# One fixed order of all steps, three copied index columns per tile and a fourth PT buffer in block-sparse attention followed by a cosine MLP

## The chip, the cores and the metric

The kernel runs on one core of one Trainium2 chip. The metric is the time of one execution on the device in microseconds (us). Before the change the median of three runs is 831.07 us, from 828.74 to 832.98. "PE" is the matrix engine (TensorE), "DVE" VectorE, "ACT" ScalarE, "POOL" GpSimd, and "SP" the queue that issues most DMAs.

## The reference

Inputs are q, k and v with batch 4, 8 heads, 768 positions and 64 columns, the sampled key blocks, and the two MLP weights (float64, 512 by 2048 and 2048 by 512).

```
scores = scale * np.matmul(q, k.transpose(0, 1, 3, 2))
mask = np.abs(blk_i - blk_j) <= 1          # blocks of 32 positions
mask = mask | (blk_i == 0) | (blk_j == 0) | (blk_i == 23) | (blk_j == 23)
# and 3 sampled key blocks for each query block
scores = np.where(mask, scores, -1000000000.0)
attn = np.exp(scores - np.max(scores, axis=-1, keepdims=True))
attn = attn / (np.sum(attn, axis=-1, keepdims=True) + 1e-09)
x = np.matmul(attn, v)                     # heads side by side: 3072 rows of 512
h = x @ w_in
out = (h * np.cos(h)) @ w_out
```

## The kernel before, in words

Each batch is cut into six tiles of 128 query rows. Five are sparse (each head sees 352 keys: its window, the two end blocks, and three sampled blocks per query block). The sixth holds the first and the last three query blocks and is dense (768 keys). Tiles are numbered 0 to 23, so tiles 5, 11, 17 and 23 are dense. Every float32 value is held as two float16 halves, high and low.

`plan_kernel` writes the work as a list of some 3200 named steps; each step issues one or more instructions on one engine. For a tile `n` and a unit `j` (two heads of a sparse tile, one head of a dense one), the steps are these:

- `qk` (PE, lines 1501 to 1518): scores into the one PSUM buffer `sp`. A sparse unit is one step of 24 matmuls; a dense unit is two steps, one for each half of the keys.
- `mx` twice and `nb` (DVE, L1534, L1551): the mask is added and the row maximum taken, for each half of `sp`, into one of four `P` buffers.
- `ex` twice and `ph` (ACT, L1556, L1566): the exponential, and the high float16 half into one of three `ring` buffers. `pl` (DVE, L1570) writes the low half.
- `PT` (SP, L1585): a DMA transpose from `ring` into one of three `PT` buffers.
- `pv` (PE, L1595 and L1607, dense L1621): the product with the values in one of two `V` buffers, into `xp`. It frees the `PT` buffer, and the tile's last one frees `V`.

A `V` buffer of a sparse tile is filled by three SP loads and by four indirect DMAs that POOL issues (`vi`, L1469, 96 rows each); they read the row numbers from a column of `gidx`, which is written once at the start. For every pair of tiles the MLP follows: `m` (PE, L1782, 12 matmuls a step), `ev` (ACT, L1791), `ka`, `kb`, `gm`, `gl` (DVE, L1801 to L1823), `sin` and `gh` (ACT, L1809, L1820), and `d` (PE, L1832, 6 matmuls a step). ACT loads another table whenever it goes from an exponential to a sine or back.

Each engine runs its own steps strictly in the order in which they were written out, and waits where an operand isn't there. In the kernel before that order came out of `Plan.run`: it took the table `POS` as priorities, simulated queues and engines with a cost for each step, and wrote out at each point the step that could start first, with the smaller `POS` among equals. Buffers of a class were handed out in the order of `POS`.

Of the kernel before, what the change touches and what calls it, by code (L numbers as in the profile page):

```python
# [273 lines left out]
class Val:  # L274


    def __init__(self, cls=None, t=None):
        self.cls, self.t, self.slot, self.avail = cls, t, None, 0.0
        self.ops = []
        self.parts = {}  # L280
# [11 lines left out]


class ArrayClock:


    WINDOW, COLD, UP, DOWN = 4096 / 1200.0, 1.85, 0.76, 0.38

# [1615 lines left out]
```

## Time and profile before

| | before |
|---|---|
| median of 3 runs | 831.07 us (828.74 to 832.98) |
| the profiled execution, and its span from the first to the last instruction | 824.2 us, 822.4 us |
| busy PE, DVE, ACT, POOL | 719.6, 641.1, 635.7, 107.4 us |
| DMA, all queues | 146.55 MB |

The profiled execution is one more execution than the three timed ones. Busy times count every instruction from its start to its end; matmuls overlap, so a busy PE isn't a PE at its peak. The granted clock is given as a share of 2.4 GHz; its two levels are 1.2 and 2.4 GHz. The DMA share is the mean busy share of the 16 DMA engines, and it can come out above 1.

### The profile page before, as it was taken

The numbers are of one execution on the slowest core, as the hardware profiler recorded it, in microseconds if no ns is written. First come the engines' busy times: TensorE is split into PE (matmuls) and PEld (weight loads), VectorE is DVE, ScalarE is ACT, GpSimd is POOL, SyncE is SP. The second block draws the span as 40 slices with busy tenths as digits, with TensorE's granted clock in tenths as the row PEclk, the third lists the DMA queues.
The fourth block names the chain that finished last, engine by engine and source line by source line (L and its number), as shares of the span: only waits on it lengthen the run. The fifth ranks groups of instructions, "written<-read, shape, count | busy, mean of one in ns | idle before, by whom it ended". The sixth has DMA issues, their size and how long they took to land.

```text
span 822.4 us, 23028 instructions
## 1 busy us (share of the span) xinstructions
PE 719.6 (87%) x9272; PEld 507.2 (62%) x9272; DVE 641.1 (78%) x1617; ACT 635.7 (77%) x1218; POOL 107.4 (13%) x128
## 2 busy tenths in 40 slices
PE   3537589899889856999999979999999979999998
PEld 2425467566466435767767647767586558577573
DVE  5979999999969763889878975989768957967362
ACT  3667899899868973999969985989679967977251
POOL 6232203000022022100030212000300210200000
PEclk9955689999899986999999998999999989999999
DMA  8999977954989899999997999978977997675100
GB/s 309 325 236 259 239 150 174 212 126 113 205 257 183 157 196 167 171 228 177 270 187 158 178 207 206 202 154 186 217 140 134 196 181 163 157 130 99 26 26 26
DMA packets 270299, 146.55 MB, mean 178 GB/s; under 512 B 241648, under 2 KB 241776, under 8 KB 270192
## 3 DMA queue, kind: packets, MB, share of 16 engines
q1 hardware_dynamic: 265072, 129.35, 74.3%
q0 software_dynamic: 5120, 15.73, 8.6%
q8 instruction: 72, 1.18, 0.6%
q14 instruction: 35, 0.29, 0.1%
HBM read 68.23 MB, written 12.58 MB: 98 GB/s over the span
## 4 chain that ended last, share of the span: by engine, by line
PE 37%; ACT 14%; DMA 13%; DVE 9%; issue 3%; SPq 1%; DVEq 0%; ACTq 0%
PE ph L1782 15%; PE po L1832 14%; DMA PT<-ring 7%; ACT P L1556 4%; PE xp L1607 2%; ACT ring L1566 2%; DMA W<-kn 2%; DMA scr<-n 2%; PE sp L1518 1%; DVE P L1534 1%; DMA qs<-in_q_dram 1%; ACT hs L1791 1%; DVE g L1823 1%; ACT junk L1237 1%; PE xp L1595 1%
## 5 line engine op out<-in xcount | busy, mean ns | idle before, releaser
L1782 PE MATMUL ph<-xT,w 128*128 128x256 f16 x2304 | 272.3, 277 | 8.3 <-ACT hs L1791 4.2
L1832 PE MATMUL po<-w,g 128*128 128x512 f16 x1152 | 265.6, 381 | 4.1 <-DVE kn L1848 1.6
L1782 PEld LDWEIGHTS <-w 128*128 128x128 f16 x2304 | 225.6, 99 | 45.6 <-issue 8.5
L1832 PEld LDWEIGHTS <-g 128*128 128x128 f16 x1152 | 108.7, 98 | 124.4 <-issue 4.1
L1556 ACT ACTIVATE P<-P,sm 128x352 f32<-128x352 f32 (+1 forms) x224 | 152.0, 680 | 32.3 <-DVE sm L1551 23.0
L1469 POOL DMA_INDIRECT V<-scr,gidx x80 | 91.8, 1147 | 595.0 <-PE xp L1595 278.2
L1570 DVE TENSOR_TENSOR ring<-P,ring 128x704 f16<-128x704 f32 (+1 forms) x112 | 100.5, 906 | 23.8 <-ACT ring L1566 22.7
L1534 DVE CUSTOM_DVE_ANT_1 P<-sp,bias 128x352 f32<-128x352 f32 x160 | 78.6, 519 | 35.4 <-PE sp L1507 35.1
L1791 ACT ACTIVATE hs<-ph,sm 128x512 f32<-128x512 f32 x96 | 63.0, 677 | 44.7 <-PE ph L1782 40.8
L1566 ACT CAST ring<-P 128x704 f16<-128x704 f32 (+1 forms) x112 | 86.5, 786 | 13.3 <-DMA PT<-ring 12.7
L1814 DVE SCALAR_TENSOR_TENSOR hs<-hs,sm,g 128x1024 f32<-128x1024 f32 x48 | 61.1, 1281 | 11.8 <-ACT g L1809 11.2
L1501 PE MATMUL sp<-W,U 128*128 128x192 f16 x320 | 52.5, 265 | 13.5 <-DVE sm L1534 10.7
L1823 DVE TENSOR_TENSOR g<-hs,g 128x1024 f16<-128x1024 f32 x48 | 58.6, 1223 | 6.9 <-ACT g L1820 6.8
L1809 ACT ACTIVATE g<-g,sm 128x1024 f32<-128x1024 f32 x48 | 54.7, 1145 | 11.5 <-DVE g L1805 11.2
L1595 PE MATMUL xp<-V,PT 96*32 96x64 f16 x1920 | 30.9, 203 | 35.4 <-DMA PT<-ring 35.4
L1805 DVE SCALAR_TENSOR_TENSOR g<-g,hs 128x1024 f32<-128x1024 f32 x48 | 58.3, 1218 | 0.6 <-DVE Wg L1343 0.2
L1820 ACT ACTIVATE g<-hs 128x1024 f16<-128x1024 f32 x48 | 50.4, 1051 | 8.4 <-DVE hs L1814 7.9
L1801 DVE TENSOR_SCALAR g<-hs 128x1024 f32<-128x1024 f32 x48 | 32.9, 690 | 28.0 <-ACT hs L1791 27.9
L1595 PEld LDWEIGHTS <-PT 96*32 96x32 f16 x1920 | 21.7, 102 | 51.7 <-DMA PT<-ring 43.5
L1502 PE MATMUL sp<-W,U 128*128 128x64 f16 x320 | 47.8, 205 | 0.0
L1607 PE MATMUL xp<-V,PT 128*128 128x64 f16 x960 | 46.6, 204 | 0.0
L1502 PEld LDWEIGHTS <-U 128*128 128x128 f16 x320 | 33.1, 104 | 15.5 <-issue 12.1
(164 smaller groups left out, 919.1 us busy)
## 6 DMA issues: line engine op xcount, KB each, us to landing
V<-scr SPq DMA_DIRECT2D x20, 384.0 KB, 5.1
stage<-in_k_dram SPq DMA_DIRECT2D x12, 512.0 KB
w<-in_moe_w_in_dram SPq DMA_DIRECT2D x12, 512.0 KB, 6.9
w<-in_moe_w_out_dram SPq DMA_DIRECT2D x12, 512.0 KB, 4.4
V<-scr SPq DMA_DIRECT2D x8, 768.0 KB, 6.3
scr<-n SPq DMA_DIRECT2D x21, 256.0 KB, 3.3
qs<-in_q_dram SPq DMA_DIRECT2D x20, 256.0 KB, 3.5
U<-U SPq DMA_DIRECT2D x40, 128.0 KB, 2.9
```

Of the source, the lines that this page charges most:

```text
L1469: self.nc.gpsimd.indirect_dma_start(V[:96, 2 + j, :], None, self.scr[b][:, :], bass.IndirectOffsetOnAxis(ap=self.gidx[:96, c : c + 1], axi ...
L1502: mm(spv[:, :, 96:128].rearrange("p y (n c) -> p y n c", c=hf), u, ends, start=False, stop=False)
L1534: self.nc.vector.tensor_tensor_reduce(out=self.p_view(n, Pt)[:, a].rearrange("p (n c) -> p n c", c=hf), in0=sp[:, :w].rearrange("p (n c) - ...
L1556: self.nc.scalar.activation(Pv[:, a], Pv[:, a], AF.Exp, scale=qc[:, 4:5], bias=nb[:, bcol : bcol + 1], accum_out=sums[:, 2 * j + a : 2 * j ...
L1566: self.nc.scalar.copy(R[:, :, 0, : self.width(n)], self.p_view(n, Pt))
L1570: self.nc.vector.tensor_tensor(R[:, :, 1, :w], self.p_view(n, Pt), R[:, :, 0, :w], ALU.subtract)
L1607: mm(xp[:, h, :], PT[:, 6 * a + 3 * l + c, :], V[:, c, h, d0:d1], start=False, stop=(a == 1 and c == 1 and x == len(terms) - 1),)
L1782: self.nc.tensor.matmul(ph[:, ff, :], self.W1[p][:, wl, cc, c * P : (c + 1) * P], xT[:, xl * NCC + cc, :], start=(j == 0), stop=(j == len( ...
L1791: self.nc.scalar.activation(hs[:, h * 512 : h * 512 + 512], ph.rearrange("p f t -> p (f t)"), AF.Copy, scale=self.turns[b][:, p : p + 1])
L1814: self.nc.vector.scalar_tensor_tensor(hs, hs, c[:, p : p + 1], kt, op0=ALU.mult, op1=ALU.mult)
L1823: self.nc.vector.tensor_tensor(g[:, 1024:2048], hs, g[:, 0:1024], ALU.subtract)
L1832: self.nc.tensor.matmul(po, g[:, gl, ff, t * P : (t + 1) * P], self.W2[p][:, wl, ff, :], start=(first and ff == half * hf and j == 0), sto ...
```

## The change

Four things change.

The planner's simulation is gone. `POS` now holds whole numbers, one for each of the 3262 steps, and `Plan.run` sorts the steps by them: that is the order, and a buffer that a step needs is the free one of its class that was freed longest ago. The table is new throughout.

Of a sparse tile's four gathers, three (`vi` 1 to 3) no longer read their row numbers from `gidx`. A new DVE step `gr` copies that column into a column of a new tile `gone`, one per gather, and the gather reads it there; so it waits for the copy. There are 60 such copies.

The step `mx` now also names the second half of `sp` as something that it reads, so no order can put it ahead of the second `qk` step of a dense unit. There are four `PT` buffers in place of three.

```
 POS = [
-    -30.456, -29.801, -23.939, -53.034, 166.579, -20.984, 140.138, 219.885, 227.197, 131.714, 120.363, 232.646, -27.188, -24.922, -13.735, -56.138,
+    2826, 2831, 2840, 2873, 2742, 2750, 2751, 2780, 2790, 2789, 2795, 2805, 2818, 2893, 2912, 2922, 2934, 2942, 2952, 2993, 2746, 2754, 2594, 2635,
...
+    def run(self):
+        order = sorted(self.ops, key=lambda o: (o.pos, o.n))
...
             for v in o.acq:
+                h = holder[v.cls]
+                free = [x for x in range(len(h)) if h[x] is None] or [x for x in range(len(h)) if not h[x].left]
+                x = min(free, key=lambda x: h[x].freed if h[x] else x)
+                h[x], v.t = v, self.classes[v.cls][x]
...
             for j in range(4):
-                op("POOL", 1.03, ipos + 0.8 + j * 0.5, lambda j=j: e.v_gather(n, V.t, j), r=[scr[b], gidx], w=[(V, 10 + j)], dma=1.5, name=f"vi{n}_{j}")
+                ix = gidx
+                if j:
+                    ix = Val()
+                    op("DVE", 0.08, ipos + 0.7 + j * 0.5, lambda j=j: e.gather_ready(n, j), r=[gidx], w=[ix], name=f"gr{n}_{j}")
+                op("POOL", 1.03, ipos + 0.8 + j * 0.5, lambda j=j: e.v_gather(n, V.t, j), r=[scr[b], ix], w=[(V, 10 + j)], dma=1.5, name=f"vi{n}_{j}")
...
-                   r=[(sp, a), bias if sparse else dbias], w=[(Pt, a), (mx, a)], name=f"mx{n}_{j}_{a}")
+                   r=[(sp, a), (sp, 1), bias if sparse else dbias], w=[(Pt, a), (mx, a)], name=f"mx{n}_{j}_{a}")
...
-        qs=[None], U=[None] * 2, P=[None] * 4, ring=[None] * 3, PT=[None] * 3, V=[None] * 2,
+        qs=[None], U=[None] * 2, P=[None] * 4, ring=[None] * 3, PT=[None] * 4, V=[None] * 2,
...
+    def gather_ready(self, n, j):
+        c = 4 * self.seq[n][1] + j
+        self.nc.vector.tensor_copy(self.gone[:96, 3 * n + j - 1 : 3 * n + j], self.gidx[:96, c : c + 1])
...
-            bass.IndirectOffsetOnAxis(ap=self.gidx[:96, c : c + 1], axis=0),
+            bass.IndirectOffsetOnAxis(ap=self.gone[:96, 3 * n + j - 1 : 3 * n + j] if j else self.gidx[:96, c : c + 1], axis=0),
```

The order differs on every engine. Three places show how.

**PE, from the scores of unit 1 of tile 8 to its values.** Each row is the first matmul of a step; the rest of the step is left out. `sp<-W,U` is a `qk`, `xp<-V,PT` a `pv`, `po<-w2,g` a `d`. Before:

```order
L1501 MATMUL sp0_115<-W_63,U0_94 128x2x96
...
L1595 MATMUL xp1_117<-V0_106,PT1_104 32x64
...
L1595 MATMUL xp1_117<-V0_106,PT2_105 32x64
...
L1595 MATMUL xp0_116<-V1_107,PT0_103 32x64
...
L1501 MATMUL sp0_115<-W_63,U1_95 128x2x96
...
L1595 MATMUL xp0_116<-V1_107,PT1_104 32x64
```

The first row stands for three `qk` steps in a row (units 1, 2 and 3 of tile 8), and the last is the `pv` of unit 1: six steps of attention stand from the one to the other, and no step of the MLP. Now, at the same place, its first nine steps and its end (the `qk` rows after the first read like it and are left out):

```order
L1299 MATMUL sp0_117<-W_63,U0_95 128x2x96
...
L1393 MATMUL xp0_118<-V0_108,PT1_105 32x64
...
L1630 MATMUL po1_123<-w2_1_69,g2_87 128x512
...
L1393 MATMUL xp0_118<-V0_108,PT2_106 32x64
...
L1393 MATMUL xp1_119<-V1_109,PT0_104 32x64
...
L1630 MATMUL po0_122<-w2_1_69,g2_87 128x512
...
L1630 MATMUL po1_123<-w2_2_70,g1_86 128x512
...
L1393 MATMUL xp0_118<-V0_108,PT3_107 32x64
```

From the first row to the last there are now six `qk`, seven `pv` and ten `d` steps; the `PT` buffers in use are four.

**POOL, the gathers of tile 10.** Waits are shown: PE stands for the `V` buffer, DVE for a copy, DMASW for an earlier gather. Before:

```order
L1469 DMA V1_107<-scr1_123,gidx_73 96x1024 [waits DMASW7_49,DMASW4_49,PE_49]
L1469 DMA V1_107<-scr1_123,gidx_73 96x1024 [waits DMASW5_49,PE_49]
L1469 DMA V1_107<-scr1_123,gidx_73 96x1024 [waits DMASW6_49]
L1469 DMA V1_107<-scr1_123,gidx_73 96x1024
```

Now:

```order
L1267 DMA V0_108<-scr1_125,gidx_73 96x1024 [waits DMASW6_49,DMASW4_49,PE_49]
L1267 DMA V0_108<-scr1_125,gone_74 96x1024 [waits DMASW5_49,DMASW7_49,DVE_49,PE_49]
L1267 DMA V0_108<-scr1_125,gone_74 96x1024 [waits DVE_49,PE_49]
L1267 DMA V0_108<-scr1_125,gone_74 96x1024
```

Two of the four wait for a copy by DVE as well.

**DVE, at the scores of unit 3 of tile 10, the change alone.** The copy that the third gather waits for stands here, between the two rounding steps of the MLP and ahead of the two maxima of that unit (`ISA P<-sp,bias`):

```order
L1599 TENSOR_SCALAR g_86<-hs_84 128x1024
L1368 TENSOR_TENSOR ring_101<-P_97,ring_101 128x2x352
L1042 RECIPROCAL sm<-sm 128x1
L1261 COPY gone<-gidx 96x1
L1603 SCALAR_TENSOR_TENSOR g_86<-g_86,hs_84 128x1024
L1332 ISA P_97,sm<-sp_117,bias 128x352
```

Before, there is no copy at all, and nothing on DVE that a gather waits for.

## Rows read from the trace of the kernel before

**Rows 1.** The page's first part: busy us, share of the span, instructions.

```profile
PE 719.6 (87%) x9272; PEld 507.2 (62%) x9272; DVE 641.1 (78%) x1617; ACT 635.7 (77%) x1218; POOL 107.4 (13%) x128
```

**Rows 2.** Windows view, stretches in us: busy us by engine, clock, DMA share, GB/s.

```profile
0.00:50.00 50.00, 22.53 (x267) 18.49 (x268) 38.52 (x112) 28.30 (x54) 26.46 (x56) 0.93 0.94 315
50.00:100.00 50.00, 27.32 (x568) 21.07 (x568) 44.96 (x123) 37.01 (x84) 9.22 (x8) 0.61 1.09 232
100.00:150.00 50.00, 44.99 (x735) 34.17 (x736) 47.64 (x116) 45.74 (x84) 7.74 (x4) 0.87 0.79 183
150.00:200.00 50.00, 46.91 (x465) 33.52 (x465) 48.74 (x98) 44.27 (x78) 0.00 (x0) 1.00 0.71 151
200.00:250.00 50.00, 43.63 (x358) 28.84 (x357) 41.56 (x106) 38.43 (x75) 7.43 (x6) 0.93 0.84 206
250.00:300.00 50.00, 43.11 (x665) 27.17 (x663) 41.56 (x136) 44.55 (x107) 5.55 (x6) 1.00 0.91 177
300.00:350.00 50.00, 35.86 (x658) 29.16 (x659) 29.27 (x85) 31.38 (x64) 8.34 (x8) 0.76 1.05 167
350.00:450.00 100.00, 99.81 (x1058) 69.89 (x1056) 85.64 (x213) 89.73 (x171) 8.80 (x8) 1.00 0.94 205
450.00:500.00 50.00, 43.63 (x850) 28.29 (x849) 39.49 (x129) 44.57 (x100) 9.99 (x10) 0.95 1.06 194
...
650.00:700.00 50.00, 44.84 (x758) 33.63 (x748) 33.02 (x91) 36.39 (x76) 4.04 (x4) 0.93 0.96 175
```

**Rows 3.** Chain of waits, 280 to 330 us: start, us, what.

```profile
288.65 0.36 PE xp L1595 x24
289.01 0.46 PE xp L1607 x12
...
292.85 9.58 DMA PT<-ring
...
310.21 10.72 DMA PT<-ring
```

**Rows 4.** Timeline of POOL, 289 to 318 us: start, us, what, idle before.

```profile
289.31 0.91 POOL L1469 DMA_INDIRECT V<-scr,gidx  x1 [37.05 <-PE xp L1595]
...
306.69 0.91 POOL L1469 DMA_INDIRECT V<-scr,gidx  x1 [12.80 <-PE xp L1595]
```

**Rows 5.** Waits view from 150 us: us in total, times, longest.

```profile
PE xp L1595 <- DMA PT<-ring: 24.8, 12, 3.7
```

**Rows 6.** Lines view, whole span: busy us, mean ns, idle before.

```profile
L1534 DVE CUSTOM_DVE_ANT_1 P<-sp,bias 128x352 f32<-128x352 f32 x160 | 78.6, 519 | 35.4 <-PE sp L1507 35.1
L1551 DVE TENSOR_SCALAR sm<-sm 128x2 f32<-128x2 f32 x80 | 17.6, 226 | 0.8
L1556 ACT ACTIVATE P<-P,sm 128x352 f32<-128x352 f32 (+1 forms) x224 | 152.0, 680 | 32.3 <-DVE sm L1551 23.0 <-DVE sm L1549 6.9 <-DVE sm L1548 1.7
L1566 ACT CAST ring<-P 128x704 f16<-128x704 f32 (+1 forms) x112 | 86.5, 786 | 13.3 <-DMA PT<-ring 12.7
L1570 DVE TENSOR_TENSOR ring<-P,ring 128x704 f16<-128x704 f32 (+1 forms) x112 | 100.5, 906 | 23.8 <-ACT ring L1566 22.7 <-issue 0.8
L1556 ACT ACT_TABLE_LOAD x20 | 25.7, 1283 | 0.3
L1168 DVE CAST V<-V 128x1 f32<-128x1 int32 x1 | 0.2, 151 | 0.0
```

**Rows 7.** DMA view: KB each, median us from issue to landing.

```profile
PT<-ring SPq DMA_TRANSPOSE x108, 4.5
V<-scr,gidx POOLq DMA_INDIRECT x80, 5.8
```

**Rows 8.** Tile view of V: its DMAs' time to landing.

```profile
DMA to landing us min/median/max: 3.1/5.6/10.4
```

**Rows 9.** Chain of waits, whole span: start, us, what.

```profile
481.06 2.59 PE po L1832 x12
```

More of the change, by code (lines that the diff above doesn't have):

```diff
@@ L277, in __init__ @@
     def __init__(self, cls=None, t=None):
-        self.cls, self.t, self.slot, self.avail = cls, t, None, 0.0
+        self.cls, self.t = cls, t
         self.ops = []
@@ L291, in nudge_keys @@
     return [kind] + ([kind + a] if a else []) + ([f"{kind}{a}_{b}"] if b else [])
-class ArrayClock:
-    WINDOW, COLD, UP, DOWN = 4096 / 1200.0, 1.85, 0.76, 0.38
-    def __init__(self):
-        self.k, self.busy, self.warm = 0, 0.0, False
-    def run(self, t, work):
-        while work > 1e-9:
-            end = (self.k + 1) * self.WINDOW
-            if t >= end - 1e-9:
-                self.warm = self.busy >= self.WINDOW * (self.DOWN if self.warm else self.UP)
-                self.k, self.busy = self.k + 1, 0.0
-                continue
-            rate = 1.0 if self.warm else self.COLD
-            d = min(end - t, work * rate)
-            t, work, self.busy = t + d, work - d / rate, self.busy + d
-        return t
-class Queues:
-    def __init__(self):
-        self.ends = [0.0, 0.0]
-    def run(self, which, at, work):
-        other = self.ends[1 - which]
-        begin = max(at, self.ends[which])
-        if other <= begin:
-            end = begin + work
-        else:
-            shared = other - begin
-            end = begin + 2 * work if work <= shared * 0.5 else begin + shared + (work - shared * 0.5)
-            self.ends[1 - which] += (min(end, other) - begin) * 0.5
-        self.ends[which] = end
-        return end
 class Plan:
@@ L351, in op @@
         o.preds, o.succ, o.acq, o.held, o.n = set(after), [], [], [], len(self.ops)
-        o.start = o.end = o.done = None
+        o.vals = []
         for key, writes in [(k, False) for k in r] + [(k, True) for k in w]:
@@ L375, in op @@
         return o
-    def run(self, delta, stick, mstick=0.0):
-        ops = self.ops
-        queues = {c: collections.deque() for c in self.classes}
-        for o in sorted(ops, key=lambda o: (o.pos, o.n)):
-            for v in o.acq:
-                queues[v.cls].append(v)
-        heads = {q[0] for q in queues.values() if q}
-        for o in ops:
-            before = sorted(o.preds | {v.ops[0] for v in o.held}, key=lambda x: x.n)
-            o.need = len(before) + sum(v not in heads for v in o.acq)
-            for p in before:
-                p.succ.append(o)
-            o.vals = []
-        for v in {id(v): v for o in ops for v in o.acq}.values():
-            v.left, v.free_at = len(v.ops), 0.0
+    def run(self):
+        order = sorted(self.ops, key=lambda o: (o.pos, o.n))
+        for v in {id(v): v for o in order for v in o.acq}.values():
+            v.left, v.freed = len(v.ops), 0
             for o in v.ops:
@@ L394, in run @@
         holder = {c: [None] * len(t) for c, t in self.classes.items()}
-        ready = {"SP": [], "PE": [], "DVE": [], "ACT": [], "POOL": []}
-        free = dict.fromkeys(ready, 0.6)
-        dma, table, order, clock = Queues(), None, [], ArrayClock()
-        def ready_now(o):
-            t = 0.0
-            for v in o.held:
-                t = max(t, v.avail)
-            for p in o.preds:
-                t = max(t, p.done if p.dma or p.eng == o.eng == "PE" else p.done + LAT[p.eng])
-            o.floor = t
-            ready[o.eng].append(o)
@@ L408, in slot_time @@
-        def slot_time(v):
-            best = None
-            for k, h in enumerate(holder[v.cls]):
-                if h is None:
-                    return 0.0, k
-                if not h.left and (best is None or h.free_at < best[0]):
-                    best = (h.free_at, k)
-            return best
-        for o in ops:
-            if not o.need:
-                ready_now(o)
-        mode = 0
-        while len(order) < len(ops):
-            pick = None
-            for eng, cand in ready.items():
-                at = max(free[eng], dma.ends[0] - 1.75) if eng == "SP" else free[eng]
-                lim, times = 1e18, []
-                for o in cand:
-                    t = max(at, o.floor)
-                    for v in o.acq:
-                        s = slot_time(v)
-                        if s is None:
-                            t = 1e18
-                            break
-                        t = max(t, s[0])
-                    times.append(t)
-                    lim = min(lim, t)
-                if lim >= 1e18:
-                    continue
-                best = None
-                for o, t in zip(cand, times):
-                    if t > lim + delta:
-                        continue
-                    key = (o.pos + (stick if o.table and o.table != table else 0.0) + (mstick if eng == "PE" and o.mode[0] != mode else 0.0), o.n)
-                    if best is None or key < best[0]:
-                        best = (key, t, o)
-                k = (best[1], *best[0])
-                if pick is None or k < pick[0]:
-                    pick = (k, best[2])
-            if pick is None:
-                raise RuntimeError("no runnable step: " + " ".join(o.name for c in ready.values() for o in c))
-            t, o = pick[0][0], pick[1]
-            for v in o.acq:
-                v.avail, v.slot = slot_time(v)
-                v.t = self.classes[v.cls][v.slot]
-                holder[v.cls][v.slot] = v
-                q = queues[v.cls]
-                q.popleft()
-                if q:
-                    x = q[0].ops[0]
-                    x.need -= 1
-                    if not x.need:
-                        ready_now(x)
-            if o.table and o.table != table:
-                table = o.table
-                t += TABLE_LOAD
-            if o.eng == "PE":
-                if o.mode[0] != mode:
-                    t += MODE_SWITCH
-                mode = o.mode[1]
-            o.start = t
-            o.end = clock.run(t, o.cost) if o.eng == "PE" else t + o.cost
-            if o.eng == "SP":
-                h = t + o.hw
-                d = max(h + 0.65, dma.ends[0])
-                if o.hw != 0.63:
-                    o.end = h + 0.03
-                elif o.dma > 1.0:
-                    o.end = d + 0.2
-                else:
-                    o.end = h + (0.65 if o.dma > 0.5 else 0.57)
-                o.done = dma.run(0, h + 0.65, o.dma * DMA_SLOW) + DMA_DONE + o.lat
-            elif o.dma:
-                o.done = dma.run(1, o.end + 1.0, POOL_DMA) + DMA_DONE + o.lat
-            else:
-                o.done = o.end
-            free[o.eng] = o.end
-            ready[o.eng].remove(o)
-            order.append(o)
-            t = o.done if o.dma else o.done + LAT[o.eng]
@@ L489, in run @@
+        done = set()
+        for k, o in enumerate(order):
+            assert all(id(p) in done for p in o.preds | {v.ops[0] for v in o.held}), o.name
+            for v in o.acq:
+                h = holder[v.cls]
+                free = [x for x in range(len(h)) if h[x] is None] or [x for x in range(len(h)) if not h[x].left]
+                x = min(free, key=lambda x: h[x].freed if h[x] else x)
+                h[x], v.t = v, self.classes[v.cls][x]
             for v in o.vals:
                 v.left -= 1
-                v.free_at = max(v.free_at, t)
@@ L492, in run @@
-            for x in o.succ:
-                x.need -= 1
-                if not x.need:
-                    ready_now(x)
+                v.freed = k
+            done.add(id(o))
         self.order = order
-        return max(o.done for o in order)
 def plan_kernel(env, B, H, S, D, DM, DFF, pr):
@@ L1056, in __init__ @@
         self.gidx = pool.tile([96, 4 * self.NS], I32, name="gidx")
+        self.gone = pool.tile([96, 3 * len(self.seq)], I32, name="gone")
         self.bias = pool.tile([P, self.NS, 22], BF16, name="bias")
@@ L1873, in block_sparse_attention_then_cos_mlp @@
     pl = plan_kernel(env, B, H, S, D, *w_in.shape, PARAMS)
-    pl.run(PARAMS["DELTA"], PARAMS["TSTICK"], PARAMS["MSTICK"])
+    pl.run()
     with tc.manual_schedule():
```

325 rows, old and new, of the table POS are left out of this document.

## The prediction
> **What bounds the kernel now.** I read the busy times first. PE is busy for 87% of the span, DVE for 78% and ACT for 77% [rows 1]. All three are close together, and matmuls overlap, so the share alone doesn't say which of them sets the end. Next I read the table of stretches [rows 2], because the kernel has phases. In the first 150 us DVE is busy for 38.5 + 45.0 + 47.6 = 131 us, while PE is busy for 23, 27 and 45 of each 50: here the loading and splitting of weights on DVE is the limit. From 350 to 450 us PE is busy for 99.8 of 100 at full clock: here PE is the limit. Between these stand four stretches in which neither holds: 250 to 300, 300 to 350, 450 to 500 and 650 to 700. PE is idle in them for 6.9, 14.1, 6.4 and 5.2 us, together 32.6 us, while DVE and ACT are idle too. They are the passes over a batch's sparse tiles.
>
> The chain of waits says what is late there. At 292.85 and at 310.21 it runs for 9.58 and 10.72 us through one DMA transpose into a PT buffer [rows 3], where the median from issue to landing is 4.5 us [rows 7]. POOL's timeline shows a burst of four gathers starting at 289.31 and another at 306.69, each as soon as PE had given the V buffer free [rows 4]. So both long transposes ran beside a burst. From 150 us on, PE waits 24.8 us in 12 pieces for such transposes [rows 5]. The clock adds to it: in 300 to 350 the granted clock is 0.76, which with levels of 1.2 and 2.4 GHz means that half of the time was spent on the lower one, after PE had waited.
>
> The order explains why PE stands still although MLP work exists. Between the scores of unit 1 of tile 8 and its values PE has six steps, all attention. A values step takes 0.36 + 0.46 = 0.8 us [rows 3], and I price a scores step, of similar size, the same: 6 x 0.8 = 5 us of cover. What has to happen meanwhile is two maxima, a bias, two exponentials, the high half, the low half and the transpose: 2 x 0.519 + 0.226 + 2 x 0.680 + 0.786 + 0.906 [rows 6] + 4.5 [rows 7] = 8.8 us, if each engine is free at once. Other units' steps stand ahead of it on DVE and ACT, so I take 15 us as what is needed.
>
> **The change, part by part.**
>
> *The order on PE, with four PT buffers.* For the same unit PE now has six scores, seven values and ten down steps in between. A down step of 6 matmuls takes 2.59 / 2 = 1.295 us [rows 9], so the cover is 13 x 0.8 + 10 x 1.295 = 23 us. I counted all 84 units of tiles 6 to 23 in this way: before, 18 have less than 15 us and the smallest has about 4; now none has less than 15 and the smallest has 16. The MLP's own chain gains as well: the steps between an up projection and the first down projection that needs it are worth mostly 10 to 30 us before, and 20 to 40 us now. What is recoverable is the idle time of the four stretches, 32.6 us, and what the low clock took. For the latter I multiply missing clock, length and busy share: 0.24 x 50 x 0.72 = 8.6 us in 300 to 350, 0.05 x 50 x 0.87 = 2.2 in 450 to 500 and 0.07 x 50 x 0.90 = 3.1 in 650 to 700 [rows 2]; together 14 us. That makes 46.5 us. Bounds are 0 (the wait moves elsewhere) and 46.5. I take 30 us: no unit is left under the need, but DVE and ACT were busy for up to 44 of 50 us there and will stop PE at times.
>
> *The gathers.* The gathers are not fewer, so the DMA work stays. Where a copy stands late on DVE, the burst is drawn out. The excess of the two long transposes is 9.58 + 10.72 - 2 x 4.5 = 11.3 us, and most of that is already in the 46.5 us. I put 5 us on it, between 0 and 11. The Trainium skill (DMA: Bandwidth & Descriptors, "Queues, rings and completion order") states that a DMA engine takes the queues with work in turn, a packet at a time. By that a gather slows whichever transposes it meets, early or late, and drawing it out brings nothing: the gain would be 5 us smaller (805 us). The two long transposes beside the bursts [rows 3, 4] agree that they share, but no row shows what a drawn out burst does.
>
> *The copies themselves.* DVE gets 60 of them; the nearest row, a one-column cast, takes 0.151 us [rows 6]: 9 us in all. By the order 18 of them stand ahead of the maxima of tile 5's third unit, in the stretch where DVE is the limit: 18 x 0.151 = 2.7 us on the path. The rest lies beside PE. Bounds 0 and 9.
>
> *Table loads.* The order of ACT has 48 of them instead of 42: 6 x 1.283 = 7.7 us [rows 6]. They lie beside PE where ACT has slack; I take 1.4 us, between 0 and 7.7.
>
> *Maxima after both halves.* In the order before, both scores steps of every dense unit already stood ahead of its maxima, so no instruction moves because of this: 0.
>
> *The start.* SP now fetches one q tile, the indices and one weight piece ahead of most of K, and DVE begins with that work. With each step's duration in the trace, the orders put 132 us of DVE work (before) and 134 us (now) ahead of the same first 75 us of PE work, so I put 0 on it beside the copies, between a gain of 11.5 us (all of DVE's idle time in the first 50 [rows 2]) and a loss of 6 us (one transfer more ahead of K; nearest is the 5.8 us of a gather [rows 7]).
>
> The sum, on the profiled execution of 824.2 us: -30 - 5 + 2.7 + 1.4 = -30.9, so 793.3 us. The median of the runs is 831.07, 1.0083 of that execution; times this ratio the forecast is **800 us**.
>
> **Rivals.**
>
> *The gathers come late (slower).* Before, a gather waited for nothing but its V buffer, and it had much time; now its start hangs on DVE's turn. At tile 10 the copy for the third gather stands just ahead of the maxima of unit 3. On PE there follow, up to the tile's first values step, three values steps, three halves of dense scores (0.4 us each, half of a scores step), two up and three down steps (an up step priced as a down step): 3 x 0.8 + 3 x 0.4 + 5 x 1.295 = 10 us. Two issues of 0.91 us with 0.3 between them and 5.6 us to landing [rows 4, 8] make 7.7 us, but 12.5 with the longest landing. It decides as soon as DVE runs 2.5 us behind PE, or when gathers land as slowly as the slowest did. For it speaks that DVE is the busiest engine after PE; against it, that many copies stand tiles ahead of their gather and bind nothing. If 17 sparse tiles each lost 3 us, the sum would be 793 + 51 = 844, or 851 us in the median.
>
> *Nothing gained (same).* The DMA share in 300 to 350 is 1.05 [rows 2]. If the engines of the DMA are the limit there, a deeper order only moves the wait, from values to a free ring or PT buffer, and ACT and DVE stop instead. Half of this would leave the stretches around 475 and 675 us, about 13 us: 824 - 13 + 4 = 815, or 822 us. All of it would leave 828, or 835 us. Against it: the same four tiles now have more MLP steps among them, so their transfers stand over a longer time.
>
> *More is gained.* If all 46.5 us go, and with them half of the idle time and lost clock between 100 and 250 us (idle 5.0 + 3.1 + 6.4; clock 0.13 x 50 x 0.90 + 0.07 x 50 x 0.87 = 9; so 12 of 23.5 us), the sum is 824 - 46.5 - 12 + 4 = 770, or 776 us. Against it: DVE is busy for 42 to 49 of 50 us there.
>
> *The copies bind nothing.* If all 60 are done long before their gather, the bursts stay and the 5 us go: 798, or 805 us. This lies in the forecast's own range.
>
> **How the numbers follow.** The forecast, with a gain between 15 and 42 us, gets 0.62, and its own range is 788 to 815. More gained gets 0.14, half gained 0.12, nothing gained 0.05, late gathers 0.07. A measurement of this kernel can tell about 0.5%, 4 us, from no change: below 826.9 is faster, above 835.2 slower. Faster is 0.62 + 0.14 + nearly all of 0.12, or 0.86; same is 0.06; slower is late gathers and a little of nothing gained, 0.08. The range for 8 in 10 goes from 775 to 825: it takes in most of the second and third case and leaves out late gathers, no gain and the best ends.
>
> **What would show it.** Right: the stretches that hold tiles 6 to 9, 12 to 15 and 18 to 21 show PE busy for 48 or more of 50 us at a clock of 0.98 or more; the wait of PE for PT transposes from 150 us on falls from 24.8 us to less than 8; the transposes' long pieces leave the chain; ACT shows 48 table loads and DVE 60 more copies of about 0.15 us; the first 150 us look as before. Wrong: a wait of PE for V, with POOL released by DVE just before it, would show the late gathers; long waits of ACT for a ring buffer, with PE idle as before, would show that the wait has only moved; a DMA share above 1 with PE idle in those stretches would show that transfers are the limit.

## The result, and the profile after

The changed kernel's median is 808.5 us of four runs (798.9 to 819.9), beside 832.0 us for the kernel before on the same chip: a ratio of 0.960, 95% interval 0.950 to 0.970. Measured again on another chip its median is 808.3 us of six runs and the ratio 0.971 (0.965 to 0.977). So it is faster by 2.5 to 4%, where the forecast was 800 us, 3.7%. The runs of one kernel scatter by up to 2.6% here (and one run of e2_old_order_4pt took 2463 us), and the ratios leave out those that lie over 1.5% above their kernel's fastest; by the medians of all runs they would be 0.972 and 0.975. The profiled execution took 799.7 us, with a span of 797.9 us, 24.5 us less than that of before, where the sum said 30.9. The total came out close. Its parts did not, as the experiments show.

The page of the kernel after, busy times and chain by engine:

```profile
PE 712.1 (89%) x9272; PEld 500.6 (63%) x9272; DVE 641.0 (80%) x1677; ACT 644.1 (81%) x1224; POOL 128.1 (16%) x128
...
PE 45%; DVE 25%; DMA 12%; ACT 11%; issue 5%; SPq 1%; DVEq 0%; ACTq 0%
```

PE does the same 9272 matmuls in 712.1 us of busy time instead of 719.6 (87% of a longer span [rows 1]). Next the stretches, with the columns of [rows 2]:

```profile
0.00:150.00 150.00, 93.59 (x1552) 75.11 (x1553) 134.75 (x379) 111.04 (x225) 52.05 (x67) 0.77 0.94 240
...
250.00:300.00 50.00, 45.68 (x750) 28.02 (x749) 43.11 (x150) 45.76 (x102) 10.70 (x10) 0.96 1.14 205
300.00:350.00 50.00, 48.73 (x794) 36.25 (x793) 43.07 (x127) 48.20 (x97) 5.27 (x5) 1.00 1.11 207
350.00:400.00 50.00, 50.00 (x522) 36.08 (x520) 42.56 (x96) 43.70 (x81) 0.00 (x0) 1.00 0.98 203
...
450.00:500.00 50.00, 45.26 (x707) 31.46 (x705) 36.95 (x99) 41.56 (x80) 9.87 (x8) 0.97 1.09 191
...
600.00:650.00 50.00, 47.52 (x794) 35.09 (x790) 40.46 (x119) 43.20 (x88) 8.46 (x8) 0.97 1.10 189
```

The stretch 300 to 350 is filled: 48.7 of 50 us at full clock, against 35.9 at 0.76. 250 to 300 and 450 to 500 still lose 4 to 5 us each, and 600 to 650 loses 2.5; the DMA share is above 1 in all four. So the sign that the prediction named, 48 of 50 us at a clock of 0.98 or more where the sparse tiles are, is met in one of these four stretches only. PE's waits from 150 us on (us in total, times, longest):

```profile
PE sp L1299 <- DVE sm L1332: 5.3, 4, 4.4
PE xp L1405 <- issue: 3.2, 1, 3.2
PE sp L1299 <- DMA U<-U: 2.5, 1, 2.5
...
PE xp L1393 <- DMA PT<-ring: 1.3, 1, 1.3
```

The wait for PT transposes of [rows 5] fell from 24.8 us to 1.3 (5.0 in a second profile, e5_again). That wait alone doesn't measure the gain: it is 1.3 us in e1_no_copies and 10.7 in e2_old_order_4pt as well, and neither is faster than the kernel before. Nor have the transposes' long pieces left the chain: one lasts 8.07 us at 492 and one 8.32 at 611. What is left on PE waits for other transfers: the longest wait for the maxima (4.4 us, up to 247) stands behind a transpose of K that lasts 7.26 us in the chain, and the wait for U behind a piece of 7.32. The groups that the prediction named, busy time and mean of one:

```profile
L1607 ACT ACT_TABLE_LOAD x24 | 30.8, 1283 | 0.4
L1354 ACT ACT_TABLE_LOAD x23 | 29.5, 1283 | 0.3
...
L1261 DVE COPY gone<-gidx 96x1 int32<-96x1 int32 x60 | 8.0, 141 | 1.3 <-issue 1.3
```

With one more table load on another line there are 48, and 60 copies of 0.14 us, both as forecast. Which of the copies bind shows in POOL's waits, over the whole span:

```profile
POOL V L1267 <- DVE sm L1349: 41.4, 2, 26.3
...
POOL V L1267 <- DVE gone L1261: 39.7, 6, 13.7
...
POOL V L1267 <- DVE sm L1079: 6.5, 1, 6.5
```

Six of 60 copies keep a gather back by this view, together 39.7 us. The three waits of the other two rows, 47.9 us, are put down to the instruction that follows a copy on DVE: these gathers start 0.2 to 0.3 us after their copy has ended, so they hung on a copy too, all three in the first five tiles. That makes 9 of 60. Most tiles from tile 6 on still start their gathers 1.2 to 2.2 us apart.

To place the gain I match PE's 695 steps in two traces (each has all 9272 matmuls), take the usual fastest time of each kind of step, 668 us in all, and count how late PE is when it has done the same amount of work. This is the table to which the experiments come back. Each row is one profile, and two profiles of one kernel differ by up to 10 us at the start (the two of the change) and by 14 us from 220 to 560 (e1 and e11):

| PE grows later by (us), while it does its work from | 0 to 60 us | 60 to 180 | 180 to 220 (tiles 8, 9) | 220 to 560 | 0 to the end |
|---|---|---|---|---|---|
| before | 78.3 | 17.8 | 27.6 | 25.5 | 149.8 |
| changed | 77.9 | 17.1 | 7.6 | 20.6 | 124.6 |
| changed, second profile (e5_again) | 88.3 | 17.8 | 8.3 | 22.2 | 138.0 |
| old order, four buffers (e2) | 79.4 | 19.2 | 26.4 | 30.1 | 155.8 |
| old order, gathers apart (e9) | 75.4 | 17.6 | 23.1 | 19.5 | 136.2 |
| new order, no copies (e1) | 92.7 | 19.6 | 11.9 | 36.6 | 162.2 |
| new order, no copies (e11) | 91.0 | 15.6 | 10.7 | 22.2 | 140.9 |
| new order, copies from tile 6 on (e8) | 87.4 | 17.4 | 7.7 | 22.7 | 136.5 |
| new order, more distance (e10) | 85.1 | 19.1 | 6.2 | 20.5 | 132.3 |
| new order, three buffers (e3) | 84.3 | 18.5 | 12.2 | 60.2 | 176.6 |
| changed, no gathers from tile 6 on (e4) | 78.7 | 12.2 | 3.1 | 6.8 | 102.2 |

In the first profile 20 of the 25 us come from tiles 8 and 9, and 5 from the rest. In the second, tiles 8 and 9 bring 19 us again, but the start loses 10.

### The profile page after: what moved, and what is told of

Read it like the earlier page. It is cut to its first block, busy times and chain, and to the rows that moved or that the text cites. A ratio compares the mean times of both kernels' runs of the same rounds, so it can differ in the third digit from the quotient of the medians.

```text
span 797.9 us, 23153 instructions
## 1 busy us (share of the span) xinstructions
PE 712.1 (89%) x9272; PEld 500.6 (63%) x9272; DVE 641.0 (80%) x1677; ACT 644.1 (81%) x1224; POOL 128.1 (16%) x128
## 4 chain that ended last, share of the span: by engine, by line
PE 45%; DVE 25%; DMA 12%; ACT 11%; issue 5%; SPq 1%; DVEq 0%; ACTq 0%
PE ph L1580 19%; PE po L1630 18%; DMA PT<-ring 5%; DVE P L1332 4%; DVE ring L1368 3%; ACT P L1354 2%; PE xp L1405 2%; DVE w L1048 2%; PE sp L1299 2%; ACT ring L1364 1%; DMA W<-kn 1%; DMA xT<-n 1%; DVE g L1621 1%; PE sp L1316 1%; DMA scr<-n 1%
## 5 line engine op out<-in xcount | busy, mean ns | idle before, releaser
L1630 PE MATMUL po<-w,g 128*128 128x512 f16 x1152 | 272.8, 385 | 3.1 <-ACT ot L1642 1.9
L1580 PEld LDWEIGHTS <-w 128*128 128x128 f16 x2304 | 223.2, 98 | 48.5 <-issue 8.1
L1267 POOL DMA_INDIRECT V<-scr,gone x60 | 84.6, 1410 | 428.3 <-PE xp L1393 144.4
L1368 DVE TENSOR_TENSOR ring<-P,ring 128x704 f16<-128x704 f32 (+1 forms) x112 | 100.7, 903 | 19.7 <-ACT ring L1364 19.6
L1299 PE MATMUL sp<-W,U 128*128 128x192 f16 x320 | 51.6, 262 | 23.6 <-DVE sm L1332 16.9
L1618 ACT ACTIVATE g<-hs 128x1024 f16<-128x1024 f32 x48 | 50.4, 1050 | 17.4 <-DVE hs L1612 17.3
L1267 POOL DMA_INDIRECT V<-scr,gidx x20 | 29.9, 1496 | 100.6 <-DMA W<-kn 69.8
L1332 DVE CUSTOM_DVE_ANT_1 P<-sp,dbias 128x384 f32<-128x384 f32 x64 | 33.9, 550 | 10.8 <-PE sp L1316 10.0
L1354 ACT ACTIVATION_READ_ACCUMULATOR P<-P,sm 128x1 f32 x224 | 42.1, 188 | 0.0
```

Of the source, the lines that this page charges most:

```text
L1267: self.nc.gpsimd.indirect_dma_start(V[:96, 2 + j, :], None, self.scr[b][:, :], bass.IndirectOffsetOnAxis(ap=self.gone[:96, 3 * n + j - 1 : ...
L1299: mm(spv[:, :, 0:96], u, keys[:, :, 64 * i : 64 * i + 96], start=(z == 0), stop=False)
L1332: self.nc.vector.tensor_tensor_reduce(out=self.p_view(n, Pt)[:, a].rearrange("p (n c) -> p n c", c=hf), in0=sp[:, :w].rearrange("p (n c) - ...
L1354: self.nc.scalar.activation(Pv[:, a], Pv[:, a], AF.Exp, scale=qc[:, 4:5], bias=nb[:, bcol : bcol + 1], accum_out=sums[:, 2 * j + a : 2 * j ...
L1368: self.nc.vector.tensor_tensor(R[:, :, 1, :w], self.p_view(n, Pt), R[:, :, 0, :w], ALU.subtract)
L1580: self.nc.tensor.matmul(ph[:, ff, :], self.W1[p][:, wl, cc, c * P : (c + 1) * P], xT[:, xl * NCC + cc, :], start=(j == 0), stop=(j == len( ...
```

## The experiments

The theory was that of the forecast: the order, with the fourth buffer, earns nearly all, and the gathers' distance a little. The rivals: the buffer alone, the order alone, or the distance alone.

### First round: each part taken away

**e1_no_copies.** In `gather_v` and `v_gather`:

```
-                    ix = Val()
-                    op("DVE", 0.08, ipos + 0.7 + j * 0.5, lambda j=j: e.gather_ready(n, j), ...
...
-            bass.IndirectOffsetOnAxis(ap=self.gone[:96, ...] if j else self.gidx[:96, c : c + 1], axis=0),
+            bass.IndirectOffsetOnAxis(ap=self.gidx[:96, c : c + 1], axis=0),
```

> The changed kernel without its 60 copies: every gather reads the one index table, as before the change, and stands on POOL where the changed order puts it; all other instructions keep their order and the four PT buffers stay. Undisturbed runs of the changed kernel took 798.9 and 799.7 us, of the kernel before 828.7 to 833.0. Theory (the copies draw out the bursts of gathers and that is worth 5 us): 803 to 806 us, and transposes into PT of over 8 us come back into the chain between 275 and 330 us. Rival (the copies bind nothing or the burst costs nothing): 796 to 801 us, the 2.7 us of copies in the first 150 us may be won. A second rival for the start: in the changed kernel PE waits 9 us for V at 64 us, behind a copy; without copies these gathers start earlier and up to 8 us go there: 791 to 797 us.

Measured: median 837.1 us, ratio 0.9989 (0.9949 to 1.0028). None of the three expectations had this: without its copies the changed order is, on this chip, no faster than the kernel before. The chain of this kernel shows a PT transpose of 14.71 us from 476 to 491 and one into xT of 9.69 us right after it, while POOL starts eight gathers between 470 and 488.

**e2_old_order_4pt.** The table POS holds the places of the order before, without copies; `PT=[None] * 4` stays.

> The order of the kernel before on all five engines, with gathers as before and no copies, but with the fourth PT buffer. Theory (what paid is the order: more PE work between the scores of a unit and its values; the old order keeps 4 to 15 us of it for 18 units whatever the buffers): 825 to 833 us, with PE waiting some 20 us for PT transposes from 150 us on. Rival (the buffer alone lets the transposes start earlier and the order was not needed): 800 to 812 us.

Measured: median 830.8 us, ratio 0.9995 (0.9966 to 1.0025). The theory holds: the buffer alone is worth nothing in the old order.

**e3_new_order_3pt.**

```
-        ... ring=[None] * 3, PT=[None] * 4, V=[None] * 2,
+        ... ring=[None] * 3, PT=[None] * 3, V=[None] * 2,
...
-        for k, o in enumerate(order):
+        while wait:
+            (take the first step of wait whose buffers are free and whose inputs are done)
```

> The changed kernel with three PT buffers: seven steps of SP's order (five PT transposes among them) stand a few places later because a fourth buffer is not there; the orders of PE, DVE, ACT and POOL are the changed ones, and the copies stay. Theory (order and buffer work together, since values that stand later hold their buffer longer): 804 to 812 us, with PE idle around tiles 9, 13, 15, 19 and 21. Rival (the order alone did it and the fourth buffer is hardly used): 798 to 801 us.

Measured: median 852.1 us, ratio 1.0243 (1.0207 to 1.0278), slower than either kernel and far outside both expectations. Against the 0.971 of the whole change, measured on another chip, the fourth buffer is worth 5.3%, some 44 us, in this order, and nothing in the old one. SP's queue shows why. Its waits at the line that issues the PT transposes, first with three buffers:

```profile
SPq L1391 <- PE xp L1413: 44.0, 21, 6.1
SPq L1391 <- PE ph L1588: 34.9, 12, 8.4
SPq L1391 <- PE sp L1313: 20.6, 8, 8.7
```

and in the changed kernel:

```profile
SPq L1383 <- PE sp L1305: 14.6, 7, 3.4
...
SPq L1383 <- PE ph L1580: 10.8, 6, 2.7
```

Values that stand later hold their PT buffer longer. With three, SP stands at the next transpose until PE is through, and all transfers behind it in SP's order wait too: at that line SP's waits for PE add up to 149 us with three buffers and 47 with four. The table has the loss in the column from 220 to 560 (60.2 us, against 20.6 and 22.2).

**e4_no_gathers.** `if n >= 6: return` at the head of `v_gather`.

> The changed kernel without the 60 gathers of the 15 sparse tiles from tile 6 on: their V rows keep what an earlier tile left there, all else runs as in the changed kernel, copies included. It prices what the gathers still cost. Theory (the change has taken nearly all that the bursts cost; what stalls are left wait for other transfers and for ACT and DVE): 790 to 798 us. Rival (transfers are still the limit in the sparse stretches, the gathers share the DMA engines with every transpose there): 770 to 788 us, with PE idle under 1 us in each stretch of 50 us from 250 us on.

Measured: median 787.0 us (777.0 to 789.9), ratio 0.9476 (0.9434 to 0.9519). That is the upper end of the rival's range and 3 us short of the theory's. The rival's sign is nearly met: PE is idle for under 1 us in every stretch of 50 us from 300 to 750, and for 1.5 us here:

```profile
250.00:300.00 50.00, 48.49 (x876) 32.11 (x874) 44.95 (x164) 49.20 (x111) 0.00 (x0) 1.00 1.10 191
```

So the gathers still cost the change 10 to 20 us (0.960 or 0.971 to 0.9476), more than the theory allowed. The DMA share is still 1.10 where PE is busy for 48.5 us. So the share of 1 is no limit in itself; what held PE went with the gathers.

### Second round: what is it in the copies

**e5_again.** No edit.

> The changed kernel itself, unedited, beside the next three on one chip, because its first four runs stood at 798.9, 799.7, 817.4 and 819.9 us and the kernel without copies at 825 to 841: the price of the copies can only be read beside the whole change. Theory (the change is worth its 3 to 4%): 798 to 806 us where nothing disturbs it, a ratio to the kernel before of 0.96 to 0.97. Rival (the four runs were a lucky chip and the usual time is that of the two slow ones): 815 to 822 us, 0.98 to 0.99.

Measured: median 808.3 us (798.0 to 813.4), ratio 0.971 (0.9651 to 0.9769). Nearer the theory; 798 us was the good end of the scatter.

**e6_copies_early.**

```
+    for o in copies:
+        n = int(o.name[2:].split("_")[0])
+        at = next(k for k, x in enumerate(order) if x.name.startswith(f"mx{n - 2}_" if n > 1 else "const_gidx"))
+        order.insert(at + (n < 2), o)
```

> All 60 copies stay, and the gathers still read their own copied column, but each copy stands on DVE ahead of the first maximum of the tile two before its own (those of tiles 0 and 1 right behind the index table), so that no gather waits for a copy. All else as in the changed kernel. Theory (what pays is that gathers start later and apart): the time of the kernel without copies, 828 to 840 us. Rival (what pays is something else that a copied column does, such as reading indices from a tile of its own): 798 to 806 us.

Measured: median 819.2 us, ratio 0.9873 (0.9804 to 0.9942). Slower than the change on the same chip, so most of what the copies bring is the waiting, not the copying. It is not as slow as e1_no_copies was, which called for the repeat in the third round.

**e7_pads.**

```
+        self.pad = pool.tile([P, 768], F16, name="pad")
...
     def v_gather(self, n, V, j):
+        for _ in range(3):
+            self.nc.gpsimd.memset(self.pad, 0.0)
```

> No copies; instead POOL clears a small tile of its own three times ahead of every gather, by the memset of the trace (128 x 128 in 0.19 us) some 2 us, so that the four gathers of a tile start some 3.2 us apart where they now start 1.2 us apart. Theory A (any distance between the gathers does): 798 to 812 us. Theory B (it is not the distance in general, but that single gathers are kept back until certain other transfers are through, as the order was searched with them): 822 to 838 us, like the kernel without copies. Late gathers would show as PE waiting for V.

Measured: median 808.6 us, ratio 0.9743 (0.9685 to 0.9801). Theory A: a distance that knows nothing of the order (3.4 to 4 us from gather to gather) does as much as the searched copies, although the pads cost DVE 30 us (the last section).

**e8_copies_from_tile6.** `if j and n < 6:` makes no copy.

> The copies of tiles 0 to 4 are gone (their gathers read the index table and start when V is free), those of tiles 6 to 22 stay. Without any copies PE was 15 us late by the end of the first 60 us of its work and a further 22 us late by the end, of which 7 in tiles 6 to 9 and 16 in tiles 12 to 16. Theory (the two prices are separate): about 15 us above the changed kernel, 812 to 820 us. Rival (the copies at the start only move a loss that DVE has there anyway): 798 to 806 us.

Measured: median 813.7 us, ratio 0.9861 (0.9793 to 0.993): about 1.5% above the change, as the theory had it. That is where the new order without any copies stands in the third round (0.9869), and where e6_copies_early stands on the same chip (0.9873). So by the ratios the copies of the first five tiles bring nearly all, and those from tile 6 on nothing that can be measured in this order. The single profiles of the table don't show it: this kernel's (136.5 us late) is no later than that of the change on the same chip (138.0).

### Third round: the missing corner

**e9_old_order_spread.** The old order as in e2_old_order_4pt, copies from tile 6 on; POS puts each on DVE where the trace of before shows DVE 3.3 us after the last gather.

> The missing corner: the order of the kernel before on PE, DVE, ACT and SP, four PT buffers, and from tile 6 on a copy ahead of three of a tile's gathers, each put on DVE where the trace of the kernel before shows DVE about 3.3 us after the gather ahead of it, so that the bursts of four in 5 us become 12 to 14 us long; no copies in the first five tiles. The old order with the buffer alone stood at 0.9995 of the kernel before, the new order without copies at 0.9989, the new order with gathers apart at 0.971 (copies) and 0.974 (pads). Theory A (drawing out the gathers pays by itself): 800 to 815 us, 0.965 to 0.98, with the stretches 300 to 350 and 450 to 500 us of PE filled. Theory B (only order, buffer and distance together pay, since the old order has no PE work to bridge a transpose): 822 to 832 us, 0.99 to 1.0. Slower is possible where a last gather comes late, at tile 22 above all.

Measured: median 812.2 us, ratio 0.9837 (0.9789 to 0.9886). The time lies in Theory A's range and the ratio just above it: the distance pays 1.6%, 13 us, without any new order. Theory A's sign did not come: in 300 to 350 and 450 to 500 PE is busy for 43.4 and 42.7 us. The old order without copies was measured on another chip (e2, 0.9995). POOL's timeline and the chain where [rows 3, 4] stood:

```profile
286.32 0.92 POOL L1277 DMA_INDIRECT V<-scr,gidx  x1 [25.70 <-PE xp L1403]
288.39 0.92 POOL L1277 DMA_INDIRECT V<-scr,gone  x1 [1.15 <-DVE gone L1271]
293.77 1.15 POOL L1277 DMA_INDIRECT V<-scr,gone  x1 [4.46 <-issue]
297.30 1.37 POOL L1277 DMA_INDIRECT V<-scr,gone  x1 [2.38 <-DVE gone L1271]
```

```profile
280.55 5.08 DMA PT<-ring
...
298.64 4.03 DMA PT<-ring
304.30 7.41 DMA PT<-ring
```

The four gathers of this tile start over 11 us instead of 4, and the pieces of 9.58 and 10.72 us are 4 to 7 us long.

**e10_spread.** The changed order; POS moves the copies from tile 6 on so that gathers are 3.3 us apart, and the gather without a copy goes first.

> The changed kernel, orders of PE, DVE, ACT and SP untouched, with its copies of the tiles from 6 on moved on DVE so that each gather starts 3.3 us after the one ahead of it, where its tile's first values leave 9 us; the gather that has no copy goes first in its tile. In the changed kernel itself tiles 8, 9, 14, 15, 16 and 22 still start theirs 1.2 to 1.7 us apart, and leaving the gathers out altogether stood at 0.948. Theory A (distance is what pays and more of it pays more): 785 to 799 us, 0.95 to 0.965. Theory B (the places that the search found are as good as the distance): 800 to 812 us, 0.965 to 0.98.

Measured: median 801.7 us (800.1 to 807.1), ratio 0.9693 (0.9651 to 0.9736). Theory B: the interval holds the 0.971 of the change, so more distance than it has brings nothing that can be measured.

**e11_no_copies_again.** As e1_no_copies.

> The changed order without copies once more, on the chip of the two kernels above, because its first runs reached from 825 to 841 us. Theory (bursts cost this order its whole gain): 825 to 840 us, 0.99 to 1.005. Rival (the first measurement was a poor chip, and early copies at 0.987 are the truer price): 812 to 822 us, 0.98 to 0.99.

Measured: median 818.3 us, ratio 0.9869 (0.9835 to 0.9904), on another chip the rival's value. The two intervals of one kernel don't meet: 1.2% lie between two chips, so a smaller difference between chips means nothing here. It agrees with e6_copies_early. POOL's timeline at the start shows what the copies do there. Without them:

```profile
47.28 2.21 POOL L1266 DMA_INDIRECT V<-scr,gidx  x1 [26.99 <-DMA w<-in_moe_w_in_dram]
...
56.86 1.52 POOL L1266 DMA_INDIRECT V<-scr,gidx  x1 [0.30 <-issue]
58.68 0.92 POOL L1266 DMA_INDIRECT V<-scr,gidx  x1 [0.30 <-issue]
```

and in the chain of the same kernel

```profile
58.16 15.16 DMA w<-in_moe_w_out_dram
```

and in the changed kernel:

```profile
46.85 2.08 POOL L1267 DMA_INDIRECT V<-scr,gone  x1 [26.32 <-DVE sm L1349]
49.24 1.33 POOL L1267 DMA_INDIRECT V<-scr,gidx  x1 [0.30 <-issue]
50.88 2.97 POOL L1267 DMA_INDIRECT V<-scr,gone  x1 [0.31 <-issue]
54.16 1.03 POOL L1267 DMA_INDIRECT V<-scr,gone  x1 [0.31 <-issue]
63.62 2.49 POOL L1267 DMA_INDIRECT V<-scr,gone  x1 [8.43 <-DVE gone L1261]
```

Eight gathers start in 12 us, the last of them beside the load of a weight piece, which then takes 15.16 us, and DVE, which is the limit here, waits 5.2 us for it. One copy holds POOL for 8.4 us in the change, and no such wait of DVE is left. It is there in all four kernels whose first gathers wait for no copy (4.5 to 8.4 us in e1, e6, e8, e11), and it is gone or 1.8 us long in the five profiles with these copies (the change twice, e3, e4, e10). In the first 150 us DVE does 122.5 us of work without copies and 134.8 in the first profile of the change, but only 125.7 in the second.

### Last: a better start?

**e12_old_start.** POS: the first 924 steps of the old order's whole list, up to the values of tile 5 on PE, where the two orders have 16 steps that differ, then the rest in the order of e10_spread.

> The order of the kernel before for the first 924 steps of the whole list (all engines, up to the values of tile 5 on PE; these gathers without copies), then the changed order with the spread copies of e10_spread; four PT buffers. In the profiles PE had lost 84 to 86 us by the end of its first 120 us of work in the old order (80 with spread copies later on), and 85, 94, 95 and 99 us in the changed order (the change, e10_spread, the change again, without copies). Theory (the changed start is no better than the old one and its losses scatter more): old start and new rest add up to 119 to 124 us lost on PE, against 124.6 in the best profile of the change and 132 in e10_spread: 794 to 799 us, a ratio of 0.955 to 0.964. Rival (the start's transfers land on the sparse tiles whatever the order, so that nothing is won): 800 to 808 us, 0.966 to 0.976.

Measured: median 811.2 us, ratio 0.9794 (0.9733 to 0.9855): the rival's side, and worse than it. The old start did bring PE to 120 us of work 82.0 us late instead of the 93.8 of e10_spread, but from there to 160 us it lost 23 us where e10_spread lost 8.5. Whether that is the seam or the transfers was not tried. No version beat the change by more than can be measured.

## Why the prediction was right, and where its parts were wrong

Ratios to the kernel before in one table; "apart" is whatever keeps the gathers apart:

| | gathers in bursts | apart from tile 6 on | apart in all tiles |
|---|---|---|---|
| old order | 1; 0.9995 with four buffers | 0.9837 (e9) | not run |
| new order, four buffers | 0.9989, 0.9869; 0.9873 with copies that nobody waits for | 0.9861 (e8) | 0.960, 0.971 (the change); 0.974 (pads), 0.969 (spread) |

- *The order on PE, with four PT buffers* (30 us): the step that was too large. On a like footing order and buffer bring 0 to 11 us with bursts, and with gathers apart from tile 6 on nothing that can be measured (0.9837 to 0.9861). From 0.9837 to the 0.971 or 0.960 of the change it is 11 to 20 us, but there the first five tiles have copies too, and the old order with gathers apart in all tiles was not run, so how much of this is the order's stays open. The mechanism stands in tiles 8 and 9: 26 to 28 us late there in the old order with bursts, 11 to 12 in the new one with bursts, whatever the rest does. That is 15 us, where the cover is 23 us instead of 5. Two things failed. The other idle time of 250 to 300, 450 to 500 and 650 to 700 was counted as recoverable: in the row from 220 to 560 the new order with bursts (22.2 and 36.6) is no better than the old (25.5 and 30.1), as far as two profiles of each can tell. And the start of the new order was priced at 0 (below), where it takes back up to 13 of the 15. That the buffer belongs to the order, as the step had it, was right: 0 in the old one, 44 us in the new.
- *The gathers* (5 us, 0 to 11): too small. 13 us by the old order (0.9995 to 0.9837), from tile 6 on; 13 by the new (0.987 to 0.971), by the ratios all of it from the first five tiles (0.9861 without these copies); and 23 against the first measurement without copies. The step failed where it said that most of the long transposes' excess "is already in the 46.5 us": it booked a loss that the bursts made on the order. From tile 6 on the two remedies replace each other and do not add up: the distance brings 13 us in the old order and, in the new one, nothing that can be measured. The step also looked at two transposes only; a weight load and transposes of K, x and U came late beside bursts as well. The rule of the Trainium skill that was set against it (DMA: Bandwidth & Descriptors, "Queues, rings and completion order": engines take the queues with work in turn) gave 0, and the runs speak against what I drew from it. Turns may well be taken, as the 14.71 us transpose beside eight gathers suggests. My reading, which no run shows by itself, is that PE bridges four transposes that are each a little late and not one that is very late.
- *The copies themselves* (2.7 us): 60 of 0.141 us, 8.0 us on DVE where 9 was worked out, and with nobody waiting for them (0.9873) the same as none at all (0.9869): 0 on the path, within what can be told.
- *Table loads* (1.4 us): 48 of 1.283 us as forecast. No run took them apart, so their share stays open.
- *The start* (0): too good. Where the first tiles' gathers wait for no copy the new order is 87 to 93 us late after 60 us of work (e1, e8, e11), where the old one is 75 to 79 (before, e2, e9); with the copies it is 78 to 88 (the change twice, e3, e4, e10). So the new start costs some 13 us, and the copies give back part of that, 7 us between the means. The 0 was right in the best profiles only.
- *Rivals.* Late gathers did not come where they were expected: from 150 us on PE waits for V for 0.9 us in the second profile and not at all in the first. At the start they did: there PE waits for gathers for 9.1 us in the first profile and 16.9 in the second. Without copies it waits 10.0 us there too, for the loads of V by SP (e11). "Nothing gained" because of the DMA share fell with e4_no_gathers.

So two errors met: the order at least 10 us too high, the gathers at least 8 us too low. The range held because both were drawn from the same idle time; that the total came within 9 us of the forecast was in part luck.

## What to carry to other kernels

When an engine waits for a transfer, look at what another queue started in those microseconds, and try to make that wait before reordering the work that suffers: the distance between gathers was worth 1.6% in the old order with nothing else changed but a fourth buffer that brings nothing there. Price a buffer only together with the order that uses it. Two remedies for one wait can replace each other, so measure each with and without the other. And book each idle microsecond once, on the part whose removal an experiment could show.

## What was not expected

A POOL memset slows some of DVE's instructions. The rows show DVE's copies of gathered K columns and its two-column bias, first in the changed kernel, then in e7_pads, which has no copies and adds 184 us of memsets on POOL:

```profile
L1137 DVE COPY Wg<-W 128x256 f16 x116 | 17.2, 220 | 1.2 <-PE sp L1305 0.9 <-issue 0.2
...
L1349 DVE TENSOR_SCALAR sm<-sm 128x2 f32<-128x2 f32 x80 | 17.0, 221 | 0.6
```

```profile
L1136 DVE COPY Wg<-W 128x256 f16 x116 | 33.7, 492 | 0.4 <-PE sp L1306 0.4
...
L1350 DVE TENSOR_SCALAR sm<-sm 128x2 f32<-128x2 f32 x80 | 31.8, 413 | 0.6
```

Both take about twice as long on average (220 and 222 ns in e1_no_copies, which differs from e7_pads by the memsets alone), while the large subtractions keep their 0.90 us; DVE's total rises from 638.8 us (e1) to 668.7. Second, PE stood 3.0 to 4.6 us in the middle of a values step for nothing that the profile shows ("issue"), at 451 us beside a burst in the changed kernel, and likewise in e5_again, e6_copies_early, e8_copies_from_tile6 and e11_no_copies_again. It is the same matmul each time, the 5333rd of 9272; ahead of it PE stands for 2.1 us with pads, 0.5 with more distance (e10) and 0.7 without the gathers (e4). So the place belongs to the program, and bursts go with a longer stall. In each of the five a 16 KB transfer on the queue that the page calls instruction starts during the stall or less than 0.5 us ahead of it. Whether PE waited for that was not tried, so the cause is not shown.
